# Attention and a routed MoE on one core: conditions nested, block products back to back, three weight loads moved

## The chip, the cores and the metric

The kernel runs on one core of one Trainium2 chip. The metric is device time in microseconds (us) of one launch. Five engines run side by side, each with its own stream of instructions: PE (TensorE, the matrix products), DVE (VectorE), ACT (ScalarE), POOL (GpSimd) and SP (SyncE, which here only issues DMA transfers). They wait for one another through semaphores.

## The reference

Local and global attention (4 batches, 8 heads, 512 local and 32 global rows, head size 64) gives 2176 rows of 512 numbers. These rows go through a mixture of 8 experts; each row goes to one expert, up to `capacity` rows for each.

```python
logits = x @ w_gate
expert_idx = np.argmax(logits, axis=1)
gate_w = probs[np.arange(N), expert_idx]
# row i becomes row counts[e] of its expert's disp[e], while counts[e] < capacity
h = np.maximum(np.einsum('ecd,edf->ecf', disp, w1), 0.0)
y = np.einsum('ecf,efd->ecd', h, w2)
out[i] = gate_w[i] * y[expert_idx[i], pos[i]]
```

`w1` is 512 x 1024 and `w2` 1024 x 512 for each expert.

## The kernel before

Up to about 140 us a planner with hand-written costs places the attention; the change doesn't touch it. Behind it come the experts, in a stretch where the order written in the code is the order on each engine (`tc.manual_schedule()`). How many rows an expert has is known only at run time, so an expert is coded as blocks of 128 rows, 3 for expert 0 and 4 for every other, and block `i` > 0 runs only under the condition `nb[e] > i`, where `nb[e]` is read from the table of counts. Block 0 always runs. The first two blocks of rows of expert 0 that were ready earlier (`y1`) are done ahead of this.

With the inputs of this case the blocks that run are 2, 3, 2, 3, 2, 1, 4, 1 for experts 0 to 7: 18 in all. The row counts of the trace agree: 576 products with `wl` at 32 a block.

Products are made of 16-bit halves. A weight w becomes `wh` (its rounded value) and `wl` (the rest), x and h likewise. A block is two products:

- `up(e, i)`: two groups of 48 matmuls, each into one PSUM tile `pa` of the ring `psA` (5 tiles, handed out in code order, counting blocks that don't run). Behind each group `relu` writes `hh` on ACT (L990) and `hl` on DVE (L991), which frees the tile. Each matmul has a weight load of its own, so an `up` is 192 instructions on PE.
- `down(e, i)`: 24 matmuls (48 instructions) into a tile `py`, then `scale` on DVE (L998, even i) or ACT (odd i) into the row buffer `ys`, then `send`, an indirect DMA of POOL that scatters the rows to the output.

Beside this run the preparations for later experts. `w_next(k)` issues a load of 1 MB raw weights on SP (chunk k belongs to expert k // 4). `split(n)` takes n halves of chunks: `wh` on ACT (L933), then `wl` on DVE (L934), eight halves for an expert, and a `w_next` behind each second one. The buffers of `wh`, `wl` alternate between two experts, so the first half for expert e+1 can be written only after the last product of expert e-1. `gather(e)` collects the rows of expert e by indirect DMAs of POOL (L945) into `xg`, and `turn(e)` transposes them by DMAs of SP (L963) into `xT`. `count(e)` reads `nb[e]`.

In the kernel before, every `up` and `down` of a block i > 0 has a condition of its own (`guard`, L1048), and the products are staggered: `down(e, i+1)` stands behind `up(e, i)`, and `down(e-1, 0)` behind `up(e, n-1)`, where n is the coded number of blocks. A condition that isn't met is a jump on each engine; the jumped part also raises the semaphores that its instructions would have raised, once the engine's own earlier work is done.

Of the kernel before, what the change touches and what calls it, by code (L numbers as in the profile page):

```python
# [9 lines left out]
F32 = mybir.dt.float32  # L10
# [4 lines left out]
ET = mybir.EngineType  # L15
PSUM = bass.MemoryType.PSUM

B, H, SL, SG, HD = 4, 8, 512, 32, 64
S = SL + SG
NTOK = B * S  # L20
DM, FF, NE = 512, 1024, 8
HP = H // 2
NT = 20
# [874 lines left out]
def experts(tc, weigh, head, ident, x16d, sidx, gslot, didx, cnts, w1, w2, ws, w_split, wp0, rp, out):  # L898
    nc = tc.nc
    with ExitStack() as ctx:  # L900
# [18 lines left out]
        def w_next(k):  # L919
            if 0 <= k < 4 * NE:  # L920
                w_load(k // 4, k % 4)
# [19 lines left out]
        def flag(i, engines):  # L941
            return nc.values_load(cnts[0:1, i:i + 1], engines=engines, min_val=0, max_val=1)  # L942
# [28 lines left out]
        def gemm1(ps, wt, x, ft):  # L971
            wh, wl = wt
            m = 0
            for kc in range(4):
                s = slice((kc % 2) * FF + 128 * ft, (kc % 2) * FF + 128 * ft + 128)
                for wx, xi in ((wh, 0), (wh, 1), (wl, 0)):
                    nc.tensor.matmul(ps, wx[:, kc // 2, s], x(2 * kc + xi), start=(m == 0), stop=(m == 11))  # L977
                    m += 1

        def wide(py, wt, h):  # L980
            wh, wl = wt
            m = 0
            for ft in range(8):
                s = slice((ft % 4) * DM, (ft % 4) * DM + DM)
                for i, wx in ((0, wh), (1, wh), (0, wl)):
                    nc.tensor.matmul(py, h(i, ft), wx[:, 2 + ft // 4, s], start=(m == 0), stop=(m == 23))  # L986
                    m += 1

        def relu(hh, hl, ps):
            nc.scalar.activation(hh, ps, AF.Relu)  # L990
            nc.vector.scalar_tensor_tensor(out=hl, in0=ps, scalar=0.0, in1=hh, op0=ALU.max, op1=ALU.subtract)  # L991

        def scale(yo, e, i, py, n=128):
            gs = gslot[0:n, NBLK * e + i:NBLK * e + i + 1]
            if i % 2:
                nc.scalar.activation(yo[0:n], py[0:n], AF.Copy, scale=gs)
            else:
                nc.vector.tensor_scalar_mul(yo[0:n], py[0:n], gs)  # L998

        def store(src, idx):  # L1000

            r = nc.gpsimd.indirect_dma_start(  # L1002
                out=out[:, :], out_offset=IndirectOffsetOnAxis(ap=idx, axis=0), in_=src, in_offset=None,
                bounds_check=NTOK - 1, oob_is_err=False,
            )
            tc.declare_no_dep(r.ins, group="rows", reason="each token's row is written once")
            tc.add_to_no_dep_group("rows", r.ins)

        def send(yo, e, i, n=128):
            store(yo[0:n], sidx[0:n, e, i:i + 1])  # L1010

        def hidden(name):
            return [hpool.tile([128, 8, 128], F16, tag=f"h{x}", name=f"h{x}{name}") for x in "hl"]
# [3 lines left out]
        def blocks(e):  # L1017
            return 3 if e == 0 else 4

        def up(e, i):  # L1020
            H[e, i] = hidden(f"{e}_{i}")

            def work():
                for g in range(2):
                    ps = psA.tile([128, 4, 128], F32, tag="a", name="pa")
                    for f in range(4):
                        gemm1(ps[:, f, :], ws[e], lambda k: xT[e][:, k, 128 * i:128 * i + 128], 4 * g + f)
                    f = slice(4 * g, 4 * g + 4)
                    relu(H[e, i][0][:, f, :], H[e, i][1][:, f, :], ps[:])

            guard(e, i, work)

        def down(e, i):
            yo = yos[(4 * e + i) % len(yos)]

            def work():
                py = psY.tile([128, 512], F32, tag="y", name="py")
                wide(py, ws[e], lambda x, ft: H[e, i][x][:, ft, :])
                scale(yo, e, i, py)

            guard(e, i, work)
            send(yo, e, i)

        def guard(e, i, work):
            if i == 0:
                work()
            else:
                with tc.If(nb[e] > i):  # L1048
                    work()

        todo = []
        yos = [yp.tile([128, DM], F32, name=f"ys{i}", bufs=1) for i in range(6)]
# [1 line left out]
        def split(n):  # L1054
            for e, c, h in todo[:n]:
                w_half(e, c, h)
                if h:
                    w_next(4 * e + c + 6)
            del todo[:n]
# [5 lines left out]

        def expert(e):

            n = blocks(e)
            if e + 1 < NE:
                w_pair(e + 1)  # L1070
                todo.extend((e + 1, c, h) for c in range(4) for h in range(2))
            for i in reversed(range(n)):
                up(e, i)
                split(1)
                if i == n - 1:
                    if e:
                        down(e - 1, 0)
                        if e == 1:
                            for j in range(HEAD):
                                store(y1[j][:], head["sidx"][:, j:j + 1])  # L1080
                    if e == 2:
                        with tc.If(flag(2 * NE, (ET.Pool,)) > 0):
                            for t in range(NT):
                                store(zero[:], didx[:, t:t + 1])
                    if e + 2 < NE:
                        gather(e + 2)
                        count(e + 2)
                else:
                    down(e, i + 1)
                    if i == 0 and e + 2 < NE:  # L1090
                        turn(e + 2)
                split(1)
            split(len(todo))

        def beyond(e):
            M = CAP - ROWS
# [20 lines left out]
            send(yo, e, 4, M)  # L1117

        with tc.manual_schedule():
            for k in range(4, 9):  # L1120
                w_next(k)
            gather(0)
            turn(0)
            gather(1)
            nc.gpsimd.memset(zero, 0.0)
            for t in yos:
                nc.gpsimd.memset(t, 0.0)
            weigh(None)
            y1 = []
            for i in range(HEAD):  # L1130
                py = psY.tile([128, 512], F32, tag="y", name="py")
                wide(py, ws[0], lambda x, ft: head["hl" if x else "hh"][:, ft, 128 * i:128 * i + 128])
                if i == 0:
                    weigh(psY.tile([128, 2, NE * NBLK], F32, tag="y", name="tg"))
                y1.append(yp.tile([128, DM], F32, tag=f"yo{i}", name=f"yo{i}", bufs=1))
                nc.vector.tensor_scalar_mul(y1[i], py, head["gslot"][:, i:i + 1])
            count(0)
            count(1)
            turn(1)
            w_next(9)  # L1140
            for e in range(NE):
                expert(e)
            down(NE - 1, 0)
            with tc.If(flag(2 * NE + 1, ALL) > 0):
                for e in range(NE):
                    beyond(e)
# [93 lines left out]
```

## Time and profile before

| | us |
|---|---|
| three runs | 391.24, 384.72, 389.38 |
| median | 389.38 |
| the profiled execution, device time | 386.15 |
| its span (first to last instruction) | 384.4 |
| PE busy | 332.4 (86%) |
| DVE busy | 221.6 (58%) |
| ACT busy | 186.4 (48%) |
| POOL busy | 174.2 (45%) |

The profiled execution is 1.75 us longer than its span and 3.2 us below the median. The trace gives for each engine the instructions with start and duration, and for an idle time the engine or transfer whose event ended it ("<-"); "PEq" and "DVEq" are the engines' sequencers, whose branch instructions don't count as busy.

### The profile page before, as it was taken

The page shows a single profiled execution, that of the slowest core. Times are in us where ns is not written, and L with a number is a line of the kernel's source. Part 1 is how long each engine was busy: PE and PEld are TensorE (multiplying, and loading weights), DVE is VectorE, ACT ScalarE, POOL GpSimd, SP SyncE. Part 2 cuts the span into 40 slices and gives each one's busy share as a digit, 9 for nine tenths or more (in the row PEclk, how much of TensorE's full clock was granted, in tenths as well). Part 3 has the DMA queues.
Part 4 walks back from the last instruction along what each step waited for, and adds up shares of the span by engine and source line. Part 5 has one row for each costly group of instructions (what it writes and reads, how often), then busy time and mean ns, then how long its engine had stood idle before and what let it go on. Part 6 is the DMA issues. An engine that isn't in the chain of part 4 may idle for free. (4 is left out here: it accounts for less than half of the span.)

```text
span 384.4 us, 12011 instructions
## 1 busy us (share of the span) xinstructions
PE 332.4 (86%) x4788; PEld 230.6 (60%) x4788; DVE 221.6 (58%) x679; ACT 186.4 (48%) x369; POOL 174.2 (45%) x235
## 2 busy tenths in 40 slices
PE   6978997897988999499999999999997399999870
PEld 2455565575565785295777594975673397776540
DVE  3678979979788976333654373642672643342220
ACT  2778988778858722034542552623443433333100
POOL 8657878777575143074661126530251720200410
PEclk9799989999998999789999999999999599999996
DMA  8999895556464649759999776746399940000100
GB/s 215 286 242 362 195 262 143 142 173 211 113 196 138 106 128 398 202 110 292 235 388 319 180 272 198 254 143 147 139 374 212 341 71 2 35 21 29 59 7 9
DMA packets 62730, 70.61 MB, mean 184 GB/s; under 512 B 33598, under 2 KB 41918, under 8 KB 62656
## 3 DMA queue, kind: packets, MB, share of 16 engines
q1 hardware_dynamic: 57232, 60.32, 56.6%
q0 software_dynamic: 5280, 8.93, 6.6%
q8 instruction: 52, 0.85, 0.9%
q10 hardware_dynamic: 144, 0.33, 0.3%
q14 instruction: 22, 0.18, 0.2%
HBM read 59.06 MB, written 13.11 MB: 188 GB/s over the span
## 5 line engine op out<-in xcount | busy, mean ns | idle before, releaser
L977 PE MATMUL pa<-xT,wh 128*128 128x128 f16 x1152 | 102.4, 223 | 19.4 <-DVEq L1048 10.0
L977 PEld LDWEIGHTS <-wh 128*128 128x128 f16 x1152 | 91.2, 100 | 24.3 <-DVEq L1048 11.0
L977 PE MATMUL pa<-xT,wl 128*128 128x128 f16 x576 | 101.1, 223 | 0.0
L934 DVE SCALAR_TENSOR_TENSOR wl<-raw,wh 128x1024 f16<-128x1024 f32 x56 | 67.8, 1223 | 54.9 <-ACT wh L933 31.0
L1002 POOL DMA_INDIRECT out_dram<-ys,sidx x31 | 39.9, 1289 | 115.6 <-DVE ys L998 54.4
L933 ACT ACTIVATE wh<-raw 128x1024 f16<-128x1024 f32 x56 | 57.2, 1049 | 23.0 <-PE py L986 20.4
L990 ACT ACTIVATE hh<-pa 128x512 f16<-128x512 f32 x36 | 21.5, 596 | 91.3 <-PE pa L977 87.5
L986 PE MATMUL py<-wh,hh 128*128 128x512 f16 x176 | 64.1, 379 | 1.1
L986 PE MATMUL py<-wl,hh 128*128 128x512 f16 x160 | 60.6, 379 | 0.0
L237 POOL COPY vt<-vt 32x520 f32<-32x520 f32 (+1 forms) x80 | 52.2, 652 | 13.4 <-DMA vt<-in_v_dram 8.4
L977 PEld LDWEIGHTS <-wl 128*128 128x128 f16 x576 | 57.8, 100 | 0.0
L986 PEld LDWEIGHTS <-hh 128*128 128x128 f16 x336 | 32.6, 98 | 40.8 <-issue 4.0
L986 PE MATMUL py<-wh,hl 128*128 128x512 f16 x144 | 54.6, 379 | 0.0
L991 DVE SCALAR_TENSOR_TENSOR hl<-pa,hh 128x512 f16<-128x512 f32 x36 | 24.7, 689 | 49.6 <-ACT hh L990 47.6
L945 POOL DMA_INDIRECT xg<-x16d,sidx x31 | 33.0, 1064 | 36.4 <-DMA xT<-xg 17.9
L277 ACT ACTIVATE P<-P,nb 128x128 f32<-128x128 f32 x128 | 43.3, 394 | 9.8 <-DVE nb L270 9.2
L261 PE MATMUL s<-kbd,qt 128*32 128x256 f32 x512 | 37.8, 420 | 4.2 <-DMA kbd<-in_k_dram 2.2
L270 DVE CUSTOM_DVE_ANT_0 P<-s,cf 128x128 f32<-128x128 f32 x128 | 30.6, 283 | 9.9 <-PE s L261 9.6
L295 PE MATMUL xo<-vt,ptr 128*32 128x65 f32 x1024 | 22.1, 224 | 4.6 <-issue 2.4
L261 PEld LDWEIGHTS s<-kbd,qt 128*32 128x32 f32 x512 | 15.5, 117 | 16.6 <-issue 6.6
L323 POOL TENSOR_TENSOR x<-x,x 128x512 f16<-128x512 f32 x14 | 17.9, 1277 | 14.9 <-ACT x L320 13.3
L295 PEld LDWEIGHTS xo<-vt,ptr 128*32 128x32 f32 x1024 | 17.4, 111 | 9.6 <-issue 4.4
(152 smaller groups left out, 412.6 us busy)
## 6 DMA issues: line engine op xcount, KB each, us to landing
raw<-in_w_dram SPq DMA_DIRECT2D x32, 1024.0 KB, 7.1
vt<-in_v_dram SPq DMA_DIRECT2D x16, 390.0 KB, 5.1
kbd<-in_k_dram SPq DMA_DIRECT2D x32, 168.0 KB, 5.0
qt<-in_q_dram SPq DMA_DIRECT2D x16, 256.0 KB, 5.3
x16d<-x SPq DMA_DIRECT2D x16, 256.0 KB, 2.5
x16d<-x16g SPq DMA_DIRECT2D x32, 8.0 KB, 3.0
xg<-x16d,sidx POOLq DMA_INDIRECT x31, 5.4
out_dram<-ys,sidx POOLq DMA_INDIRECT x31, 4.6
```

Of the source, the lines that this page charges most:

```text
L237: eng.tensor_copy(dst, src)
L261: nc.tensor.matmul(s[32 * c:32 * c + 32, 2 * i:2 * i + 2, :], qt[u][:, 32 * t:32 * t + 32], kt[u][:, :, o:o + 128], start=True, stop=True,)
L270: nc.vector.tensor_tensor_reduce(out=P[u, g][:, j, :], in0=ps["s", u, g][:, j, :], in1=mask[:, 2 * g + j // 2, :], scale=-0.125, scalar=3e ...
L277: nc.scalar.activation(p, p, AF.Exp, scale=-1.0, bias=ps["nb", u, h][:, j:j + 1])
L295: nc.tensor.matmul(x[cs, j, :], ps["pt", u, g][:, j, cs], vt[u][:, w, j % 2, :], start=True, stop=True)
L933: nc.scalar.activation(wh[:, c, s], raw[e, c][:, s], AF.Copy, scale=SW)
L934: nc.vector.scalar_tensor_tensor(out=wl[:, c, s], in0=raw[e, c][:, s], scalar=SW, in1=wh[:, c, s], op0=ALU.mult, op1=ALU.subtract)
L945: nc.gpsimd.indirect_dma_start(out=dst[0:n], out_offset=None, in_=x16d[:, :], in_offset=IndirectOffsetOnAxis(ap=sidx[0:n, e, i:i + 1], axi ...
L977: nc.tensor.matmul(ps, wx[:, kc // 2, s], x(2 * kc + xi), start=(m == 0), stop=(m == 11))
L986: nc.tensor.matmul(py, h(i, ft), wx[:, 2 + ft // 4, s], start=(m == 0), stop=(m == 23))
L991: nc.vector.scalar_tensor_tensor(out=hl, in0=ps, scalar=0.0, in1=hh, op0=ALU.max, op1=ALU.subtract)
L1002: r = nc.gpsimd.indirect_dma_start(out=out[:, :], out_offset=IndirectOffsetOnAxis(ap=idx, axis=0), in_=src, in_offset=None, bounds_check=N ...
```

## The change

Each expert now has one nest of conditions: `nb[e] > 1` outermost, inside it `nb[e] > 2`, inside it `nb[e] > 3`; on the way out stand `up` and `down` of the block, back to back (`more`, whose conditions show as L1040). Block 0 follows with `up(e, 0)` and `down(e, 0)`. The sends of blocks 3 to 1, `gather(e+2)` and `count(e+2)` stand between `more` and `up(e, 0)`, and so does `ahead(e+1)`, which marks on PE where the next expert's conditions may be announced. The splits are taken as 2, 2, 3 and 1 instead of one by one. Of the five raw loads ahead of expert 0's gathers and transposes, three now stand behind its transposes.

```diff
-            guard(e, i, work)
+        def more(e, i):
+
+            if i < blocks(e):
+                with tc.If(nb[e] > i, label=f"b{e}_{i}"):
+                    more(e, i + 1)
+                    up(e, i)
+                    down(e, i)
+
+        def ahead(e):
+            if e < NE:
+                for i in range(1, blocks(e)):
+                    tc.mark_branch_hint_location(f"b{e}_{i}", hint=nb[e] > i, engines=[ET.PE])
...
-            for i in reversed(range(n)):
-                up(e, i)
-                split(1)
-                if i == n - 1:
-                    if e:
-                        down(e - 1, 0)
...
-                else:
-                    down(e, i + 1)
-                    if i == 0 and e + 2 < NE:
-                        turn(e + 2)
-                split(1)
-            split(len(todo))
+            split(2)
+            more(e, 1)
+            split(2)
+            for i in reversed(range(1, blocks(e))):
+                send(row(e, i), e, i)
...
+            if e + 2 < NE:
+                gather(e + 2)
+                count(e + 2)
+            ahead(e + 1)
+            up(e, 0)
+            if e + 2 < NE:
+                turn(e + 2)
+            split(3)
+            down(e, 0)
+            send(row(e, 0), e, 0)
+            split(1)
...
         with tc.manual_schedule():
-            for k in range(4, 9):
+            for k in range(4, 6):
                 w_next(k)
             gather(0)
             turn(0)
+            for k in range(6, 9):
+                w_next(k)
             gather(1)
...
             for e in range(NE):
                 expert(e)
-            down(NE - 1, 0)
```

SP around the transposes of expert 0, before (L44 and L47 are the raw loads, L963 the transposes):

```order
L44 DMA raw_1_3280<-in_w_dram 128x2x1024
L47 DMA raw_2_3282<-in_w_dram 128x4x512
L47 DMA raw_3_3284<-in_w_dram 128x4x512
L44 DMA raw_0_3286<-in_w_dram 128x2x1024
L963 DMA_TRANSPOSE xT_3288<-xg_2_3291 128x8x128
L963 DMA_TRANSPOSE xT_3288<-xg_1_3290 128x8x128
L963 DMA_TRANSPOSE xT_3288<-xg_0_3289 128x8x128
```

The same place on SP after:

```order
L44 DMA raw_1_3280<-in_w_dram 128x2x1024
L963 DMA_TRANSPOSE xT_3282<-xg_2_3285 128x8x128
L963 DMA_TRANSPOSE xT_3282<-xg_1_3284 128x8x128
L963 DMA_TRANSPOSE xT_3282<-xg_0_3283 128x8x128
L47 DMA raw_2_3303<-in_w_dram 128x4x512
L47 DMA raw_3_3305<-in_w_dram 128x4x512
L44 DMA raw_0_3307<-in_w_dram 128x2x1024
```

Three loads, 3 MB, have passed from ahead of the transposes to behind them.

DVE from expert 4 to expert 5, before (the digit behind a name is the expert, the next one the block or chunk; L991 is relu's half, L934 the split's, L998 `scale`):

```order
L934 SCALAR_TENSOR_TENSOR wl5_5830<-raw5_3_5539,wh5_5829 128x1024
L1048 COMPARE_AND_BRANCH
L991 SCALAR_TENSOR_TENSOR hl5_3_6442<-pa_6444,hh5_3_6441 128x512
L991 SCALAR_TENSOR_TENSOR hl5_3_6442<-pa_6495,hh5_3_6441 128x512
L1048 UNCONDITIONAL_BRANCH x2
L934 SCALAR_TENSOR_TENSOR wl6_6440<-raw6_0_5680,wh6_6439 128x1024
L998 TENSOR_SCALAR ys4_3274<-py_6548,gslot_67 128x512
L1064 TENSOR_LOAD cnts_69
L934 SCALAR_TENSOR_TENSOR wl6_6440<-raw6_0_5680,wh6_6439 128x1024
L1048 COMPARE_AND_BRANCH
```

The same place on DVE after:

```order
L998 TENSOR_SCALAR ys4_3274<-py_6466,gslot_67 128x512
L934 SCALAR_TENSOR_TENSOR wl5_5884<-raw5_3_5672,wh5_5883 128x1024
L934 SCALAR_TENSOR_TENSOR wl6_6500<-raw6_0_5846,wh6_6499 128x1024 x2
L1040 COMPARE_AND_BRANCH x3
L991 SCALAR_TENSOR_TENSOR hl5_3_6511<-pa_6512,hh5_3_6510 128x512
L991 SCALAR_TENSOR_TENSOR hl5_3_6511<-pa_6563,hh5_3_6510 128x512
```

`scale` of `down(4, 0)`, the last split half for expert 5 and the first two for expert 6 now all stand ahead of DVE's first condition of expert 5; before, one split half and a condition alternated.

PE at the border of experts 4 and 5, before (L986 is `down`, L977 `up`):

```order
L986 MATMUL py_6399<-wl4_5220,hh4_1_6151 128x512
L1048 UNCONDITIONAL_BRANCH x2
L1048 COMPARE_AND_BRANCH
L977 LDWEIGHTS wh5_5829
L977 MATMUL pa_6444<-xT5_5357,wh5_5829 128x128
```

PE after: first the row ahead of `up(4, 0)` and then, 240 rows on, the border itself:

```order
L986 MATMUL py_6258<-wl4_5268,hh4_1_6154 128x512
L1040 UNCONDITIONAL_BRANCH x2
L1063 TENSOR_LOAD cnts_69
L1063 ISA x2
L1048 REGISTER_ALU
L1236 BRANCH_PREFETCH_HINT
L977 LDWEIGHTS wh4_5267
```

```order
L986 MATMUL py_6466<-wl4_5268,hh4_0_6347 128x512
L1040 COMPARE_AND_BRANCH x3
L977 LDWEIGHTS wh5_5883
L977 MATMUL pa_6512<-xT5_5683,wh5_5883 128x128
```

There is one announcement (BRANCH_PREFETCH_HINT) for each of experts 1 to 7, for the outermost condition and one block of products ahead of it; the two inner conditions have none, nor has expert 0. The three comparisons stand together at the border.

## Rows read from the trace of the kernel before

**Rows 1.** Five stretches of the span from the end of the work ahead of expert 0 to the end: start and end, length, then busy us and instructions of PE, PEld (weight loads), DVE, ACT and POOL, the granted clock of PE, the busy share of the DMA engines, GB/s.

```profile
155.79:161.48 5.69, 0.00 (x0) 0.00 (x1) 3.11 (x3) 0.00 (x0) 0.00 (x0) 0.74 0.83 180
161.48:295.85 134.37, 130.43 (x1440) 93.80 (x1440) 65.42 (x68) 54.76 (x68) 55.09 (x51) 0.99 0.80 233
295.85:304.12 8.27, 0.00 (x0) 0.00 (x1) 6.79 (x7) 5.93 (x6) 4.29 (x4) 0.66 1.11 260
304.12:372.86 68.74, 66.24 (x720) 48.20 (x720) 23.40 (x26) 18.21 (x24) 14.79 (x13) 0.97 0.17 50
372.86:384.37 11.51, 0.00 (x0) 0.00 (x0) 0.75 (x1) 0.00 (x0) 0.98 (x1) 0.68 0.03 9
```

**Rows 2.** What PE waited for between 150 and 384 us: who waited, what ended it, us in all, how often, the longest.

```profile
PE pa L977 <- DVEq L1048: 10.0, 2, 8.3
PE pa L977 <- DMA xT<-xg: 5.7, 1, 5.7
PE pa L977 <- PEq L1048: 3.2, 6, 0.9
```

**Rows 3.** PE's instructions in order of time, those that follow a break at the start of an expert: start, duration, operation, and in brackets the idle time before it and what ended it.

```profile
161.48 0.40 PE L977 MATMUL pa<-xT,wh 128*128 128x128 f16 x2 [5.69 <-DMA xT<-xg]
...
190.97 0.27 PE L977 MATMUL pa<-xT,wh 128*128 128x128 f16 x2 [0.43 <-PEq L1048]
...
218.44 0.28 PE L977 MATMUL pa<-xT,wh 128*128 128x128 f16 x2 [0.74 <-PEq L1048]
...
273.83 0.28 PE L977 MATMUL pa<-xT,wh 128*128 128x128 f16 x2 [0.95 <-PEq L1048]
...
304.12 0.40 PE L977 MATMUL pa<-xT,wh 128*128 128x128 f16 x2 [8.28 <-DVEq L1048]
...
361.83 0.27 PE L977 MATMUL pa<-xT,wh 128*128 128x128 f16 x2 [1.77 <-DVEq L1048]
```

**Rows 4.** PE again: the first products of two `up`s of expert 6, two blocks apart, and the seam between the last `up` of expert 7 and its `down`.

```profile
322.79 0.28 PE L977 MATMUL pa<-xT,wh 128*128 128x128 f16 x2
...
343.87 0.28 PE L977 MATMUL pa<-xT,wh 128*128 128x128 f16 x2
...
367.15 0.22 PE L977 MATMUL pa<-xT,wl 128*128 128x128 f16 x1
367.52 0.38 PE L986 MATMUL py<-wh,hh 128*128 128x512 f16 x1
```

**Rows 5.** The stretches behind the two long breaks of PE, columns as in rows 1.

```profile
161.48:165.20 3.72, 3.72 (x36) 3.72 (x37) 0.00 (x0) 0.00 (x0) 1.58 (x2) 0.50 0.19 38
304.12:308.70 4.58, 4.58 (x44) 4.58 (x45) 1.04 (x1) 0.00 (x0) 3.67 (x4) 0.50 1.00 366
```

**Rows 6.** Expert 0's supply in order of time: SP's issues of the three loads that the change moves and of the transposes (SPq), then POOL's first and third gather; then two stretches, columns as in rows 1; last, over all transfers of `xg` from 140 to 200 us, the time from issue to landing.

```profile
141.63 1.38 SPq L47 DMA_DIRECT2D raw<-in_w_dram  x2
143.05 1.83 SPq L44 DMA_DIRECT2D raw<-in_w_dram  x1
156.73 4.03 SPq L963 DMA_TRANSPOSE xT<-xg  x3
...
146.86 1.07 POOL L945 DMA_INDIRECT xg<-x16d,sidx  x1 [2.81 <-DVE dl L460]
...
149.54 1.00 POOL L945 DMA_INDIRECT xg<-x16d,sidx  x1 [0.30 <-issue]
...
142.00:148.00 6.00, 6.00 (x59) 4.08 (x58) 5.33 (x27) 1.20 (x3) 2.60 (x4) 1.00 0.93 377
148.00:154.00 6.00, 6.00 (x46) 3.17 (x45) 2.46 (x10) 2.00 (x2) 2.00 (x2) 1.00 1.05 390
...
DMA to landing us min/median/max: 2.4/3.5/7.7
```

**Rows 7.** DVE around the starts of experts 5 and 7, and ACT and DVE at expert 7's last relu, columns as in rows 3.

```profile
296.75 1.22 DVE L934 SCALAR_TENSOR_TENSOR wl<-raw,wh 128x1024 f16<-128x1024 f32 x1 [3.42 <-ACT wh L933]
297.90 0.74 DVE L998 TENSOR_SCALAR ys<-py,gslot 128x512 f32<-128x512 f32 x1
298.56 1.21 DVE L934 SCALAR_TENSOR_TENSOR wl<-raw,wh 128x1024 f16<-128x1024 f32 x1
299.99 2.36 DVE L934 SCALAR_TENSOR_TENSOR wl<-raw,wh 128x1024 f16<-128x1024 f32 x2 [0.21 <-DVEq L1048]
...
360.10 0.75 DVE L998 TENSOR_SCALAR ys<-py,gslot 128x512 f32<-128x512 f32 x1 [2.55 <-PE py L986]
...
367.40 0.60 ACT L990 ACTIVATE hh<-pa 128x512 f16<-128x512 f32 x1 [2.08 <-PE pa L977]
...
368.03 0.69 DVE L991 SCALAR_TENSOR_TENSOR hl<-pa,hh 128x512 f16<-128x512 f32 x1 [1.99 <-ACTq L1048]
```

**Rows 8.** DMA packets of queue q8, which carries instructions, in the break before expert 5 (295.85 to 304.12 us) and in the 8 us that end just behind the start of expert 7 (354 to 362 us): packets, MB, share of 16 engines.

```profile
q8 instruction: 2, 0.03, 1.6%
...
q8 instruction: 2, 0.03, 1.5%
```

**Rows 9.** Expert 6's supply: POOL's last gather for it, SP's transposes of it, and the raw load that SP issues behind them.

```profile
282.11 0.99 POOL L945 DMA_INDIRECT xg<-x16d,sidx  x1 [0.31 <-issue]
...
288.89 7.22 SPq L963 DMA_TRANSPOSE xT<-xg  x4
296.21 1.50 SPq L44 DMA_DIRECT2D raw<-in_w_dram  x1
```

More of the change, by code (lines that the diff above doesn't have):

```diff
@@ L1021, in up, with row @@
             H[e, i] = hidden(f"{e}_{i}")
[L1023 to L1029, printed above, removed]
-            guard(e, i, work)
-        def down(e, i):
[L1034 to L1046, printed above, removed]
-            else:
-                with tc.If(nb[e] > i):
-                    work()
+            for g in range(2):
+                ps = psA.tile([128, 4, 128], F32, tag="a", name="pa")
+                for f in range(4):
+                    gemm1(ps[:, f, :], ws[e], lambda k: xT[e][:, k, 128 * i:128 * i + 128], 4 * g + f)
+                f = slice(4 * g, 4 * g + 4)
+                relu(H[e, i][0][:, f, :], H[e, i][1][:, f, :], ps[:])
+        def row(e, i):
+            return yos[(4 * e + i) % len(yos)]
+        def down(e, i):
+            py = psY.tile([128, 512], F32, tag="y", name="py")
+            wide(py, ws[e], lambda x, ft: H[e, i][x][:, ft, :])
+            scale(row(e, i), e, i, py)
+        def more(e, i):
[8 more added lines that the diff above has]
+                    tc.mark_branch_hint_location(f"b{e}_{i}", hint=nb[e] > i, engines=[ET.PE])
         todo = []
@@ L1066, in expert @@
         def expert(e):
-            n = blocks(e)
             if e + 1 < NE:
@@ L1071, in expert @@
                 todo.extend((e + 1, c, h) for c in range(4) for h in range(2))
-            for i in reversed(range(n)):
-                up(e, i)
-                split(1)
-                if i == n - 1:
-                    if e:
-                        down(e - 1, 0)
[L1078 to L1088, printed above, removed]
-                    down(e, i + 1)
-                    if i == 0 and e + 2 < NE:
-                        turn(e + 2)
-                split(1)
-            split(len(todo))
+            split(2)
[3 more added lines that the diff above has]
+                send(row(e, i), e, i)
+            if e == 1:
+                for j in range(HEAD):
+                    store(y1[j][:], head["sidx"][:, j:j + 1])
+            if e == 2:
+                with tc.If(flag(2 * NE, (ET.Pool,)) > 0):
+                    for t in range(NT):
+                        store(zero[:], didx[:, t:t + 1])
+            if e + 2 < NE:
[9 more added lines that the diff above has]
+            split(1)
         def beyond(e):
```

## The prediction

> **What bounds the kernel now.** I read the stretches first. From 161.48 us to 372.86 us PE is busy nearly all the time except for one hole of 8.27 us; ahead of it is a hole of 5.69 us, behind it a tail of 11.51 us in which only the last rows are written [rows 1]. DVE, ACT and POOL have spare time in the same stretches, about half or more. So PE sets the end of the expert stage, and a change is worth what it takes from PE's breaks, from time at the low clock, or from the moment at which PE can begin. The list of PE's waits names the breaks: 5.7 us for the transposes of expert 0, 10.0 us in two waits with DVE's sequencer named, 3.2 us in six waits for PE's own sequencer [rows 2]. PE's rows place them: 5.69 before expert 0, .43 at expert 1, .74 at expert 2, .95 at expert 4, 8.28 at expert 5 and 1.77 at expert 7 [rows 3].
>
> To size what is lost I take undisturbed work from the same trace. From 322.79 to 343.87 two blocks go by, 10.54 us each [rows 4]. An undisturbed `up` is 361.83 to 367.37, 5.52 or so, and the `down` behind it 367.52 to 372.86, 5.34 [rows 1, 3, 4]; start to end these would be 10.86, and matmuls that overlap at a seam of unlike products give .16 back at each of two seams. 18 blocks at 10.54 are 189.7 us; the stage took 211.4. [...]
>
> DVE is named for the 8.28 us, but I don't believe it. By the code order of the PSUM ring, the first group of `up(5, 0)` needs the tile that DVE passes over in the jumped `up(5, 3)`, and DVE was at 296.75 already in the split half behind that place, some 7 us before PE went on [rows 7]. What stands at this place on PE are four jumps over 480 instructions. The same four jumps stand at expert 7, where the hole is 1.77. In both stretches two packets of instructions were fetched [rows 8], while the DMA engines carried 260 GB/s around the first and a mean of 50 over the stretch that holds the second [rows 1]. So I read both holes as PE waiting for its code, dear when the DMA engines are full. At experts 2 and 4 two jumps over 240 instructions cost .74 and .95 under full traffic.
>
> **The change part by part.**
>
> *The three raw loads.* They are issued on SP at 141.63 to 143.05, ahead of the gathers, whose issues run from 146.86 to 149.54; the third lands when the first transpose goes off, at 156.73, 7.2 us after its issue [rows 6]. Meanwhile the DMA engines are full at 377 and 390 GB/s. Three loads are 3.1 MB, 8 us of that traffic. Without them a gather of about the median 3.5, or 2.4 at best, is at hand [rows 6], so the transposes go off at 152.0 to 153.0; I take 152.6, **4.1 us earlier**. The bounds are 0 (the gathers are slow for another reason) and 4.8. PE then starts at 157.4, 1.6 us after the work ahead of it ended at 155.79. A break of 1.77 at expert 7 left the clock at its high level, those of 5.69 and 8.28 didn't [rows 1, 3, 5], so **1.84 us** of low clock go too. Bounds of this part together: 0 to 6.6. The three loads themselves are wanted by the splits of experts 1 and 2, ten and more us later, behind PE work; on SP they pass only the three transposes. If they came too late, DVE would be late, not PE, up to some 3 us.
>
> *Products back to back.* `down` directly behind its own `up` could wait for relu. At expert 7 it did so before the change: the `up` ends at 367.37, `down` starts at 367.52, while `hh` of the second group was written from 367.40 to 368.00 and `hl` from 368.03 to 368.72 [rows 4, 7]. The first quarter of `down` needs the first group only. I cost this at nothing; the cover is the 2.7 us that `down` takes for its first four slices, against .60 + .69 of relu. Like products now meet nowhere inside an expert, so the seams fall from 4.1 us to none: **4.1 gained** (bounds 2 and 4.1).
>
> *The nest and its new wait.* Conditions go from two a block to one. But ahead of the first condition of an expert DVE now has `scale` of `down(e-1, 0)`, the last split half of this expert and the first two of the next. `scale` starts when `down` ends; the steps from row to row are .66, 1.15 and 1.22 for such instructions and .21 for the passage over conditions [rows 7], so DVE passes the condition .03 + .66 + 1.15 + 1.22 + 1.22 + .21 = **4.5 us after PE's last product**. Until then the jumped blocks' PSUM tiles aren't free, and queued behind the two splits on DVE are the relus of the first block that runs. Who waits is PE. With two blocks (experts 2 and 4) the first group of `up(e, 1)` has a tile and runs 2.76 us, the second waits: 4.5 - 2.76 = 1.74 each, where .74 + .30 and .95 + .30 were lost. With one block (expert 5) the first group itself waits: 4.5, and the clock may fall again; I take 1.84, between 0 (the 1.77 row) and 2.19 (the 8.28 row). At expert 7 no splits of a next expert are left: scale, one split half and the passage, about 2.4, in place of 1.77. With three blocks (1 and 3) I keep the .43 of the row at expert 1. Sum of what is lost after: 2 x 1.74 + 4.5 + 1.84 + 2.4 + 2 x .43 = **13.1**; of before, without the seams and expert 0's clock: 21.7 - 4.1 - 1.84 = 15.8. The nest gives **2.7 us**, less about 1.3 that I allow for overlaps at the borders that a break swallows.
>
> *Jumps.* The announcement covers expert 5's and 7's jump, now a single one over 726 instructions, because there the outermost condition fails. Experts 2 and 4 jump at the second condition, over 484 instructions, twice the distance of before, and unannounced. If the code takes F us to come, the loss there is the larger of 1.74 and F. The nearest rows: .95 (half the distance, full traffic) and, as far above, 8.28 (the same distance in four jumps, full traffic). I take F under 1.74, since a single jump over the same distance with idle DMA engines would be at most the 1.77 of four; F of 4 would add 2.3 at each.
>
> [...]
>
> Sum: 4.1 + 1.84 + 4.1 + 2.7 - 1.3 = 11.4 us. The profiled execution's 386.15 becomes 374.7. The three runs' median lies 3.2 above this execution, and I don't know whether the code fetches that the change shortens are what varies, so I add 2: **377 us**.
>
> **The rivals.**
>
> *A. The long unannounced jumps at experts 2 and 4 wait for code.* For it: the two holes with packets in them, full traffic at both places. Against it: .95 at 240 instructions. At F = 4, half of 8.28 since one jump stands for four, 2 x 2.3 = 4.6 more, and about 1 more at experts 1 and 3, if those also cost .95: 382 to 383.
>
> *B. The waits only move.* The gathers land late for another reason, the gain at the start is 0 to 2, and the wait for DVE at the borders eats the rest: 377 + 4 to 6, plus up to 4 when the clock falls at experts 2 and 4 too: 382 to 387. For it: the gathers' longest 7.7 is a property of many rows; against it, the full DMA engines in just those 6 us.
>
> *C. Slower: raw loads come late behind the transposes of SP.* `turn(e+2)` waits for `gather(e+2)`, which on POOL now stands behind the sends of blocks 3 to 1, and these wait for their `scale`. Each SP transfer behind it, the raw loads of `split(3)`, waits along. Before, the last gather for expert 6 was issued at 282.11, the transposes went off from 288.89, and the raw load behind them at 296.21 [rows 9]. The gathers move back by up to one block, 10.5 us; I find 3 to 4 us of slack for expert 6's raw load. It decides for slower only when it is late by more than 11 us, or when both jumps of A cost 8.28: then 2 x 6.5 = 13 of the 11.4 are lost, 388 to 392.
>
> *D. It doesn't do what it says*: only the outermost condition is announced, and if that has no effect the hole at expert 5 stays 8.28 instead of 4.5, and its clock 2.19: 4.1 more, 381.
>
> *E. Better:* DVE gets to the splits sooner, expert 5's break is short enough to keep the clock, and code is no matter: 370 to 373.
>
> **How the numbers follow.** Two per cent of 389.4 is 7.8 us, about what a measurement of this kernel can tell from no change; faster means under 381.6, slower over 397.2. Chances: the forecast .42 (373 to 381), E .10, D .10 (379 to 383), A .20 (380 to 385), B .12 (382 to 387), C .06 (388 to 400). Faster: .42 + .10 + half of D .05 + a fifth of A .04 = .61; slower: only the far end of C, with what I have overlooked, .05; same .34. The range leaves out the better half of E and C: 371 to 387.
>
> **What would show it.** In the changed kernel's rows: the third gather lands by 153, PE starts expert 0 at 157 to 158 with the clock at its high level; no break between `up` and its `down`; at experts 2 and 4 a break of 1.7 in the middle of the first `up` that DVE ends; at expert 5 a break of 4.5 in place of 8.28. A break ahead of the first `up` of experts 2 and 4, ended by PE's sequencer and with instruction packets in it, would be A. A transposed tile or a split that PE waits for would be C. It is wrong if the announced jump still costs 8 us, or if gathers at the start land 7 us after issue with less traffic.

## Result and profile after

In 20 interleaved runs each, the changed kernel took 382.61 us (median, 374.1 to 389.06) and the kernel before 387.14 us (384.22 to 391.3). The ratio is **0.9745, 95% interval 0.9694 to 0.9796**. The ratio compares only the runs within 1.5% of each kernel's fastest, 6 of 20 for the changed kernel and 18 of 20 for the kernel before, so it says 9.9 us where the medians of all runs say 4.5. The forecast was 377, with a range of 371 to 387. On two other chips the same kernel gave 0.9824 (0.9746 to 0.9902) and 0.9779 (0.9707 to 0.9851); there the medians fell by 8.1 and 5.7 us.

The profiled execution took 381.53 us, its span is 379.6 where it was 384.4. The stretches that answer to [rows 1], columns as there:

```profile
158.63:160.62 1.99, 0.00 (x0) 0.00 (x0) 0.82 (x2) 0.00 (x0) 0.00 (x0) 1.00 1.08 103
160.62:296.57 135.95, 129.25 (x1440) 93.84 (x1440) 65.86 (x69) 54.31 (x68) 59.18 (x51) 0.99 0.77 239
296.57:300.88 4.31, 0.00 (x2) 0.01 (x1) 4.15 (x4) 3.83 (x4) 2.94 (x2) 1.00 0.27 62
300.88:368.13 67.25, 65.21 (x720) 47.70 (x720) 26.62 (x29) 19.99 (x26) 17.06 (x15) 0.97 0.37 106
368.13:379.60 11.47, 0.00 (x0) 0.00 (x0) 0.75 (x1) 0.00 (x0) 0.98 (x1) 0.69 0.03 9
```

The work ahead of expert 0 ended 2.84 us later than in the trace of before (158.63 against 155.79), in a part that the change doesn't touch. From there the break ahead of expert 0 fell from 5.69 to 1.99, the stage of the experts from 211.38 to 207.51, and the tail is the same. 2.84 - 3.70 - 3.87 - .04 = -4.77, which is the 4.8 between the spans.

PE's waits after, to hold against [rows 2]:

```profile
PE pa L977 <- DVEq L1040: 6.3, 2, 4.3
PE pa L977 <- PEq L1040: 4.7, 3, 2.3
PE pa L977 <- DMA xT<-xg: 2.0, 1, 2.0
PE pa L977 <- issue: 1.8, 2, 1.6
```

And where they are, against [rows 3] (start, duration, operation, idle time before it and what ended it):

```profile
160.62 0.23 PE L977 MATMUL pa<-xT,wh 128*128 128x128 f16 x1 [2.00 <-DMA xT<-xg]
...
183.81 0.22 PE L977 MATMUL pa<-xT,wh 128*128 128x128 f16 x1 [0.30 <-PEq L1040]
...
186.51 0.23 PE L977 MATMUL pa<-xT,wl 128*128 128x128 f16 x1 [1.59 <-issue]
...
219.48 0.22 PE L977 MATMUL pa<-xT,wh 128*128 128x128 f16 x1 [2.12 <-PEq L1040]
...
222.50 0.22 PE L977 MATMUL pa<-xT,wl 128*128 128x128 f16 x1 [0.24 <-issue]
...
275.33 0.22 PE L977 MATMUL pa<-xT,wh 128*128 128x128 f16 x1 [2.28 <-PEq L1040]
...
300.88 0.28 PE L977 MATMUL pa<-xT,wh 128*128 128x128 f16 x1 [4.31 <-DVEq L1040]
...
357.41 0.23 PE L977 MATMUL pa<-xT,wh 128*128 128x128 f16 x1 [2.04 <-DVEq L1040]
```

These are experts 0, 1 (twice), 2 (twice), 4, 5 and 7. Expert 1, which jumped once over 242 instructions, stops .30 at its start and 1.59 more after 1.11 us of its first `up`; the second stop waits for nothing that the profile shows. I read it as missing code; no run shows that by itself. Experts 2 and 4 stop for 2.12 and 2.28 where they stopped for .74 and .95. Expert 5 stops for 4.31 instead of 8.28. The seams inside a block and between blocks are overlaps now, of .16 or .17, but for one break of .15 at the jump of expert 3.

### The profile page after: what moved, and what is told of

Its sections match the earlier page's. It is cut to its first block, busy times and chain, and to the rows that moved or that the text cites. A ratio compares the mean times of both kernels' runs of the same rounds, so it can differ in the third digit from the quotient of the medians.

```text
span 379.6 us, 11865 instructions
## 1 busy us (share of the span) xinstructions
PE 326.7 (86%) x4788; PEld 229.8 (61%) x4788; DVE 220.6 (58%) x679; ACT 185.4 (49%) x369; POOL 178.5 (47%) x235
## 5 line engine op out<-in xcount | busy, mean ns | idle before, releaser
L977 PE MATMUL pa<-xT,wh 128*128 128x128 f16 x1152 | 101.9, 223 | 13.2 <-DVEq L1040 6.3
L977 PEld LDWEIGHTS <-wh 128*128 128x128 f16 x1152 | 90.9, 100 | 19.5 <-DVEq L1040 7.3
L977 PE MATMUL pa<-xT,wl 128*128 128x128 f16 x576 | 100.5, 222 | 1.8 <-issue 1.8
L934 DVE SCALAR_TENSOR_TENSOR wl<-raw,wh 128x1024 f16<-128x1024 f32 x56 | 65.5, 1220 | 36.6 <-ACT wh L933 35.2
L1002 POOL DMA_INDIRECT out_dram<-ys,sidx x31 | 37.3, 1203 | 103.1 <-ACT ys L996 45.1
L986 PE MATMUL py<-wh,hh 128*128 128x512 f16 x176 | 64.1, 379 | 0.0
L986 PE MATMUL py<-wl,hh 128*128 128x512 f16 x160 | 60.6, 379 | 0.0
L991 DVE SCALAR_TENSOR_TENSOR hl<-pa,hh 128x512 f16<-128x512 f32 x36 | 24.8, 690 | 59.0 <-ACT hh L990 56.8
L977 PEld LDWEIGHTS <-wl 128*128 128x128 f16 x576 | 57.5, 100 | 1.8 <-issue 1.8
L945 POOL DMA_INDIRECT xg<-x16d,sidx x31 | 40.6, 1310 | 36.4 <-DMA xT<-xg 18.0
L933 ACT ACTIVATE wh<-raw 128x1024 f16<-128x1024 f32 x56 | 55.2, 1046 | 4.8 <-PE py L986 3.5
L986 PEld LDWEIGHTS <-hh 128*128 128x128 f16 x336 | 32.7, 98 | 36.8
L986 PE MATMUL py<-wh,hl 128*128 128x512 f16 x144 | 54.6, 379 | 0.0
L261 PE MATMUL s<-kbd,qt 128*32 128x256 f32 x512 | 34.0, 387 | 4.1 <-DMA kbd<-in_k_dram 3.2
L261 PEld LDWEIGHTS s<-kbd,qt 128*32 128x32 f32 x512 | 14.7, 111 | 14.0 <-issue 5.9
```

Source lines behind the costliest of these rows:

```text
L261: nc.tensor.matmul(s[32 * c:32 * c + 32, 2 * i:2 * i + 2, :], qt[u][:, 32 * t:32 * t + 32], kt[u][:, :, o:o + 128], start=True, stop=True,)
L933: nc.scalar.activation(wh[:, c, s], raw[e, c][:, s], AF.Copy, scale=SW)
L934: nc.vector.scalar_tensor_tensor(out=wl[:, c, s], in0=raw[e, c][:, s], scalar=SW, in1=wh[:, c, s], op0=ALU.mult, op1=ALU.subtract)
L945: nc.gpsimd.indirect_dma_start(out=dst[0:n], out_offset=None, in_=x16d[:, :], in_offset=IndirectOffsetOnAxis(ap=sidx[0:n, e, i:i + 1], axi ...
L1002: r = nc.gpsimd.indirect_dma_start(out=out[:, :], out_offset=IndirectOffsetOnAxis(ap=idx, axis=0), in_=src, in_offset=None, bounds_check=N ...
```

## Experiments

The kernels ran in three groups of four, each group on one chip beside the kernel before. The chip of the first group was slower with everything: the kernel before took 401.9 us there. The changed kernel itself didn't run on that chip.

**The loads alone, twice.** Only the move of the three loads, on the kernel before:

```diff
-            for k in range(4, 9):
+            for k in range(4, 6):
                 w_next(k)
             gather(0)
             turn(0)
+            for k in range(6, 9):
+                w_next(k)
```

> The kernel before with the three raw loads moved behind expert 0's transposes and nothing else. Theory (the full DMA engines held up the gathers): the third gather lands 2.2 us or so after the last issue instead of 7.2, PE's break ahead of expert 0 falls from 5.7 to about 2.0, and nothing else changes; 3.7 us faster, and 1.6 more only if the clock stays high behind the shorter break: 382 to 384 where the kernel before stands at 387. Rival (the gathers are slow by themselves, or the loads are missed later): no change, 386 to 388, with a break for a split at expert 1.

Measured: 395.31 us against 401.9, ratio 0.9793 (0.9714 to 0.9871). PE's break ahead of expert 0 was 2.4, and its first `up` took 7.16, as long as the 7.17 in the trace of after, whose first 3.58 us had a clock of .55 (below).

> The loads alone. Theory A: 3 to 5 us faster than the kernel before and as much slower than the changed one. Theory B: 5 to 8 us faster than the kernel before, within 2 us of the changed one; in its trace expert 5 still has a hole of 4.5 to 8, which splits into 4.0 up to DVE's passage and a rest.

Measured in the third group: 385.53 against 387.86, ratio 0.9941 (0.9900 to 0.9983): 2.3 us, less than either theory had. The trace has the break at 1.78, the first `up` at 5.54 and this at expert 5:

```profile
298.21 0.40 PE L977 MATMUL pa<-xT,wh 128*128 128x128 f16 x2 [8.02 <-DVEq L1048]
```

In that kernel DVE took up its next split behind the conditions at 294.34, 4.1 us after PE's last product at 290.20. So of the 8.02 some 4.1 lie ahead of DVE's passage and 3.9 behind it.

**The nest alone, twice.** The changed kernel with the loads in the old order:

```diff
-            for k in range(4, 6):
+            for k in range(4, 9):
                 w_next(k)
             gather(0)
             turn(0)
-            for k in range(6, 9):
-                w_next(k)
```

> The changed kernel with its raw loads in the old order, so the nest, the order of the products and the announcements alone. Theory: the break ahead of expert 0 is 5.7 again and its first up at the low clock takes 7.4; from there the stage is 4 us shorter than before, from the seams (4) and expert 5 (4), less what the jumps at experts 1, 2 and 4 cost more (about 4): 382 to 385. Rival (loads and nest are worth something only together, because a start moved forward meets later transfers): 386 to 388.

Measured: 403.2 against 401.9, ratio 0.999 (0.9947 to 1.0034). On this chip `down` did wait for its own relu, nearly all of it in block 0 of three experts, 4.4 us in all; so it did without announcements (below), in block 0 of four experts, 6.6 us. One of these rows, from the trace without announcements:

```profile
325.71 0.39 PE L986 MATMUL py<-wh,hh 128*128 128x512 f16 x1 [1.76 <-ACT hh L990]
```

The loads alone, which keep the staggered order, have no such wait on that chip.

> The nest alone. Theory A: 3 to 5 us faster than the kernel before. Theory B: within 2 us of it, with breaks of about 1.9, 2.4 and 1.1 to 2.3 at experts 1, 2 and 4 that PE's own code ends, and no like seams.

Measured in the third group: 387.57 against 387.86, ratio 0.9988 (0.9942 to 1.0034). Twice the nest alone is worth nothing. Its trace has the forecast overlaps at every seam but one, and expert 5's hole at 4.30; and it has 1.98, 2.58 and 1.47 at experts 1, 2 and 4. The break ahead of expert 0 was 6.43, and the first `up` behind it took 8.33. The trace is of the longest of its twelve runs; its stage took 209.70.

**No announcements, twice.**

```diff
-            ahead(e + 1)
```

> The changed kernel without its announcements. Theory (the hole at expert 5 was PE fetching code, and the announcement took it away): expert 5's break grows from 4.3 to 6 to 9 us and is ended by PE's own code, expert 7's from 2.0 to 2.5 or more, experts 2 and 4 stay at 2.1 to 2.3: 2 to 5 us slower than the changed kernel. Rival (the hole was a wait for DVE all along, and the announcement does nothing): 4.3 and 2.0 as with it, the same time.

Measured: 397.78 against 401.9, ratio 0.9899 (0.9836 to 0.9961). Expert 5's break was 5.32, and just as long in the two kernels of that group that announce (nest alone, and inner conditions announced): DVE reached the condition 5.2 us after PE's last product in all three. Expert 7 had 2.04.

> The changed kernel without announcements. If announcing hides the code of the jumps at experts 5 and 7, these breaks grow by 1 us or more over those of the changed kernel and the time by 2 to 5. If DVE's passage of the conditions is what PE waits for there, PE starts within .2 us of DVE's passage with or without announcements, and the time is within 2 us of the changed kernel.

Measured in the third group, beside the changed kernel: 383.0 and ratio 0.982 (0.9755 to 0.9886), where the changed kernel had 382.14 and 0.9779. Experts 5 and 7 stop for 4.31 and 2.04, the same as with announcements. One thing differs at expert 5:

```profile
301.96 0.28 PE L977 MATMUL pa<-xT,wh 128*128 128x128 f16 x2 [4.31 <-DVEq L1040]
...
303.92 0.39 PE L977 MATMUL pa<-xT,wh 128*128 128x128 f16 x2 [1.61 <-issue]
```

PE began on DVE's passage and then stood 1.61 us; no engine or transfer is named as the one it waited for. Behind it PE started 9 or 10 matmuls in each microsecond from 304 to 309, and 17 or 18 in the two after them. In the trace of after the clock was .52 in the first 3.52 us of this `up` and 1.00 in the rest. So the slow pace lasted longer, and this first `up` took 9.80 us where the three traces of the changed kernel have 7.16. So announcing takes away at most 2.6 us at expert 5 by this trace; in the first group's trace without announcements no such stop stands there (first `up` 7.63). The times can't tell it from nothing.

**Inner conditions announced.**

```diff
                 with tc.If(nb[e] > i, label=f"b{e}_{i}"):
-                    more(e, i + 1)
+                    ahead(e, i + 1)
                     up(e, i)
                     down(e, i)
+                    more(e, i + 1)
...
```

> The changed kernel with the inner conditions behind their block instead of ahead of it (block 1, then block 2 inside, then block 3 inside that), each announced on PE one block ahead of its jump. Theory (PE waits for code where a jump over 242 or 484 instructions is unannounced): the breaks of 1.9, 2.4 and 2.3 at experts 1, 2 and 4 fall to .4 or less, expert 5 keeps the wait of 4.3 for DVE; 5 to 6 us faster than the changed kernel, and less spread from run to run. Rival (a jump costs its 2 us announced or not): the breaks move behind block 1 and the time stays.

Measured: 405.55 against 401.9, ratio 1.0016 (0.9948 to 1.0083). The rival held: the breaks at the starts of experts 1, 2 and 4 are gone, as the theory said, but wherever a jump now stands behind a block there is a new one. At expert 0 it is 1.33, at experts 1 and 3 it is 1.55, ended by DVE; at experts 2 and 4, behind block 1, it is this:

```profile
239.24 0.27 PE L977 MATMUL pa<-xT,wh 128*128 128x128 f16 x2 [1.50 <-issue]
...
301.06 0.22 PE L977 MATMUL pa<-xT,wh 128*128 128x128 f16 x1 [1.45 <-issue]
```

So PE stood 1.5 at an announced jump over 484 instructions, where it stood .8 to 2.9 at an unannounced one in the other traces. That needn't be the price of the jump: the engine that scales the block ahead passes the same condition only behind that `scale`. At expert 2 this is ACT, whose next work starts at 238.79, .45 ahead of PE; at expert 4 it is .41, and at experts 1 and 3, with DVE in ACT's place, .36 and .35. Whether PE waited for that engine or for code isn't shown. PE's waits held an item that was larger here than anywhere: stops between matmuls that nothing explains, 15.0 us in 28 (those at the jumps among them).

```profile
PE pa L977 <- issue: 15.0, 28, 1.5
```

The `up` of expert 1's block 0 (208.17 to 220.81) shows them microsecond by microsecond, columns as in rows 1:

```profile
210.00:211.00 1.00, 1.00 (x22) 1.00 (x19) 0.23 (x1) 0.00 (x0) 0.73 (x1) 1.00 0.56 184
...
212.00:213.00 1.00, 0.49 (x3) 0.13 (x2) 0.00 (x0) 0.00 (x0) 0.70 (x2) 1.00 0.75 156
213.00:214.00 1.00, 0.39 (x4) 0.23 (x4) 0.00 (x0) 0.00 (x0) 0.89 (x1) 1.00 1.04 358
214.00:215.00 1.00, 0.35 (x4) 0.23 (x5) 0.00 (x0) 0.00 (x0) 0.80 (x1) 1.00 0.90 274
215.00:216.00 1.00, 0.49 (x5) 0.15 (x3) 0.00 (x0) 0.00 (x0) 0.69 (x2) 1.00 1.06 420
...
218.00:219.00 1.00, 0.34 (x4) 0.18 (x2) 0.61 (x1) 0.35 (x1) 0.00 (x0) 0.50 0.35 112
```

PE has 22 records of matmuls in a microsecond while the DMA engines have a share of .56, and 3 to 5 in the four rows with .75 to 1.06. No engine is named as the one it waits for. I read it as code that trickles in beside full DMA engines; that is read from the coincidence, not tried by itself, and the last row, with 4 records at a share of .35, doesn't fit it.

**The changed kernel again, twice.** No edit.

> The changed kernel once more, for a second trace of it beside the others on one chip. Theory (announcements as such cost or gain at most 1 us a place): it stands 10 to 15 us below the kernel before and below the variant without announcements. Rival (PE runs out of code while the DMA engines are full, in rows of matmuls with .3 to .5 us between them, and announcing makes this worse): it stands above the variant without announcements, whose ratio to the kernel before was .990, and its trace shows such rows at experts 1, 2, 4 or 5.

Measured: 380.01 against 388.11, ratio 0.9824. By medians it stands 8.1 below the kernel before, short of the theory's 10 to 15. No rows of stops; PE lost 1.98, 3.12 and 1.47 at experts 1, 2 and 4. The low clock behind expert 0's break, which was 2.02, did not occur this time (first `up` 5.53).

> The changed kernel on one chip with its two halves and with the variant without announcements. Theory A (the start is worth about 4 us, the nest about as much): 0.978 to 0.985 of the kernel before, 3 to 5 us below the loads alone and the nest alone. Theory B (the nest gives back at the jumps of experts 1, 2 and 4 what it saves at the seams): within 2 us of the loads alone.

Measured: 382.14 against 387.86, ratio 0.9779. By medians, on that one chip: loads alone -2.3, nest alone -.3, both -5.7. The two don't add up; the 3 us between are less than the spread of each of these kernels' runs (8 to 9 us), so whether the two help one another stays open. On the chip of the first group the loads alone came to 6.6 below the kernel before, and loads and nest without announcements to only 4.1: what the nest adds isn't settled.

**The kernel before again.** No edit.

> The kernel before once more, for a trace of it on the same chip as the others. Theory (PE's code comes late when the DMA engines are full): its trace, too, has rows of matmuls with .3 to .5 us between them at some of the experts, and a hole of 5 to 9 us at expert 5; how much of this there is differs from trace to trace, by some 10 us in all. Rival (such rows belong to the nest and to the announcements): it has none, and its stage from expert 0 to the end lasts 211 us as in its first trace.

Measured: 388.52, ratio 0.9983 (0.9915 to 1.005). The rows of stops aren't there; the stage took 212.46 us and expert 5's hole was 7.97. The work ahead of expert 0 ended at 157.86.

**The kernel before with quiet DMA engines.** Chunks 6 to 11 serve in place of 12 to 31.

```diff
...
+            k = 4 * e + c
+            if k >= 12 and (e, c) not in raw:
+                raw[e, c] = raw[(6 + k % 6) // 4, (6 + k % 6) % 4]
+                return
...
```

> The kernel before without the raw loads of chunks 12 to 31: the weights of experts 3 to 7 are not fetched, and the splits take chunks that are there already, so DVE, ACT and PE do the same work on other numbers with little DMA traffic from 190 us on. Theory (the hole of 8.3 us at expert 5 is code that comes late because the DMA engines are full): it falls to the 1.8 of expert 7, the jumps at expert 4 cost .5 or less, and no rows with gaps are left: the stage is 8 to 12 us shorter. Rival (the hole is a wait for DVE's order): it stays at 5 to 8.3 us, and at most the .3 us for a split goes.

Measured: 383.26 against 388.11, ratio 0.9913 (0.9861 to 0.9965). The stage took 208.27, 4.2 less than in the kernel before on that chip, and nearly all of it is the hole at expert 5. PE and DVE there:

```profile
303.94 0.29 PE L981 MATMUL pa<-xT,wh 128*128 128x128 f16 x1 [3.99 <-DVEq L1052]
```

```profile
302.00 0.74 DVE L1002 TENSOR_SCALAR ys<-py,gslot 128x512 f32<-128x512 f32 x1
302.66 5.09 DVE L938 SCALAR_TENSOR_TENSOR wl<-raw,wh 128x1024 f16<-128x1024 f32 x4
```

The first split of DVE's row ends at 302.66 + 1.22 = 303.88, and PE starts at 303.94. Both theories were half right: 4.0 of the hole is a wait for DVE to pass a condition behind that split, and the other 3.9 to 4.4 isn't there in this run, where the DMA engines moved a mean of 41 GB/s (299.5 to 306) and not the 278 of before (295 to 306). It isn't that a helper came later: DVE's row starts 2.71 us after PE's last product here and in the trace of before, and ACT and POOL, too, stand where they stood. Code is the reading that is left to me; this run doesn't show it by itself. The jumps at expert 4 stayed at .86.

**All four splits behind the nest.**

```diff
-            split(2)
             more(e, 1)
-            split(2)
+            split(4)
```

> The changed kernel with the first two split halves behind the nest instead of ahead of it (all four behind it). Theory (DVE passes the conditions 4.3 us after PE's last product because two split halves stand ahead): DVE passes at about 2.1 us, expert 5's break of 4.3 falls to 2.1 and its first up runs at the high clock; 3 to 4 us faster than the changed kernel. Rival (code is late there anyway): the break stays over 4 us and is put down to PE's own sequencer, the time stays, or it grows where the later splits make a down wait.

Measured: 392.6 against 388.11, ratio 1.0131 (1.0036 to 1.0227): slower than the kernel before by 0.4 to 2.2%, where 3 to 4 us less than the changed kernel were forecast. What the theory said of the break at expert 5 came true to a tenth; that the clock would stay high behind it did not (first `up` 7.17, where 5.53 goes with a clock of 1.00, below):

```profile
304.87 0.75 DVE L998 TENSOR_SCALAR ys<-py,gslot 128x512 f32<-128x512 f32 x1 [1.24 <-PE py L986]
305.53 1.22 DVE L934 SCALAR_TENSOR_TENSOR wl<-raw,wh 128x1024 f16<-128x1024 f32 x1
306.96 2.36 DVE L934 SCALAR_TENSOR_TENSOR wl<-raw,wh 128x1024 f16<-128x1024 f32 x2 [0.21 <-DVEq L1040]
```

```profile
306.86 0.23 PE L977 MATMUL pa<-xT,wh 128*128 128x128 f16 x1 [2.04 <-DVEq L1040]
```

DVE passes right behind one split and PE starts with it, 2.04 us after its last product. But the four splits now stand ahead of the relus of `up(e, 0)`, and `down(e, 0)` waits for `hl` in six of the experts:

```profile
PE py L986 <- DVE hl L991: 8.9, 6, 1.5
```

Besides, the first `up` behind each of the breaks of 2.0 to 2.9 at experts 0, 2, 4, 5 and 7 took 7.1 to 7.2 here. Wherever the two splits stand, PE waits for them: ahead of the nest it costs 2.3 us at one expert, behind it 1.5 at six.

## Why the prediction was right, and where its steps failed

The direction and the range held. The sum rests on a loss of 21.7 us in the stage of before, 211.4 less 189.7. The trace of before shows its parts: 13.6 of breaks; 4.0 of clock, from first `up`s of 7.36 at expert 0 and 7.71 at expert 5, which began at a clock of .50, against 5.52 undisturbed (1.84 and 2.19 more); and a rest of 4.1, put down to seams of like products, which show breaks of .15 (at 168.99 and 179.84, say) where unlike ones overlap by .16. By the first trace of each kernel the change gave 7.6 us, 3.7 ahead of expert 0 and 3.9 behind it, where my sum had 11.4: two thirds of it. The 3.8 that are missing are mainly 2.3 at the jumps of experts 1 to 4 and 1.6 of clock behind expert 0's break. The median, 382.61, lies outside the 373 to 381 that I called likeliest and in the 380 to 385 of rival A, and the 2.3 were lost where A has its loss, most of them at expert 1. That the range held is owed to its width, too: the kernel before alone spreads over 7 us. Term by term, with the three traces of the changed kernel:

- **The raw loads, 4.1: nearly right.** The first transpose went off 7.2 us after the last gather's issue before, and 2.15 after (154.54 behind 152.39, below); with 4.05 in another trace of the changed kernel. PE's break was 1.99, 2.02 and 3.92 against 5.7, so 3.7, 3.7 and 1.8 were gained. The loads alone brought 2.4 and 1.8. In the nine traces with the loads moved the break was 1.8 to 2.4 in six and 3.9 to 4.2 in three; why the three differ is open.

```profile
154.54 4.00 SPq L963 DMA_TRANSPOSE xT<-xg  x3
...
152.39 1.00 POOL L945 DMA_INDIRECT xg<-x16d,sidx  x1 [0.30 <-issue]
```

- **The clock behind it, 1.84: wrong in two traces of three.** I argued from the 1.77 of expert 7 that a break of 1.6 keeps the clock. The break came out at 2.0 in two traces, and there it goes either way: the granted clock was .55 behind 1.99 in the one and 1.00 behind 2.02 in the other. In the third the break was 3.92 and the first `up` took 7.89, against 5.53 at the clock of 1.00.

```profile
160.62:164.20 3.58, 3.58 (x37) 3.58 (x38) 2.29 (x2) 0.00 (x0) 1.77 (x2) 0.55 1.03 366
```

```profile
160.69:164.20 3.51, 3.51 (x63) 3.51 (x64) 2.28 (x2) 0.56 (x1) 1.76 (x2) 1.00 1.05 377
```

- **Back to back, nothing: right.** In the traces of the changed kernel no `down` waited for relu; all `up` to `down` seams in the trace of after overlap by .16 or .17. It isn't safe: on the chip of the first group such waits came to 4.4 and 6.6 us in the two kernels with the nest named above. **The seams, 4.1: right.** One break of .15 is left, at the jump of expert 3.
- **The wait for DVE: right at experts 5 and 7.** Forecast 4.5 and 2.4; measured 4.31 and 2.04, and the clock (.52 in the first 3.52 us of that `up`) cost 1.64 where I took 1.84. In the trace of after DVE ends its third split at 297.28 + 3.49 = 300.77, and PE starts at 300.88:

```profile
297.28 3.49 DVE L934 SCALAR_TENSOR_TENSOR wl<-raw,wh 128x1024 f16<-128x1024 f32 x3
300.98 2.36 DVE L934 SCALAR_TENSOR_TENSOR wl<-raw,wh 128x1024 f16<-128x1024 f32 x2 [0.21 <-DVEq L1040]
```

- **The same wait at expert 4: right in form.** I had the loss there as the larger of 1.74 and F, with a break in the middle of the first `up` that DVE ends. Where the jump was short, this is what stands there, 1.08 and then .39 in the second trace:

```profile
273.40 0.27 PE L977 MATMUL pa<-xT,wh 128*128 128x128 f16 x2 [1.08 <-PEq L1040]
...
276.63 0.28 PE L977 MATMUL pa<-xT,wh 128*128 128x128 f16 x2 [0.39 <-DVEq L1040]
```

  The second break ends 4.31 after PE's last product, as at expert 5. The sum is 1.47 here, and again in the third group's nest alone (.88 and .59) and without announcements (.77 and .70): the floor is 1.47 where I had 1.74.
- **What the hole of 8.28 was: wrong by half.** I took the whole of it for code, because I had PE wait for the tile of the jumped `up(5, 3)`; the run with quiet DMA engines shows it waiting for DVE to pass the next condition, behind `scale` and one more split. The wait for DVE of 4.0 was there before the change. So the change didn't bring a new wait at expert 5; it moved the old one by .3 and took away what came on top of it. That the hole shrank to 4.3 was right for a reason that I had only in part, and so partly by luck.
- **The jumps at experts 1, 2 and 4: too cheap.** I took F under 1.74, hidden by the wait for DVE, and .43 at expert 1. The traces show 1.9, 2.0 and 1.6 lost at expert 1, 2.4, 3.1 and 2.2 at expert 2 and 2.3, 1.5 (the floor above) and 1.8 at expert 4. Expert 1 alone is 1.4 above my term; and the break of 2.21 at expert 2 was followed by a clock of .53 and a first `up` of 7.15 in one trace. This is rival A, at F = 1.1 to 2.5 and not the 4 that I gave it. By its trace in the third group this also takes a good part from the nest alone: saved at seams and at expert 5, paid at three jumps and at the clock. That it is all of why the nest alone stands at 0.999 isn't shown. Nor is it shown that these breaks are PE waiting for code: no releaser but PE's own sequencer, or none, is named, the jumps at expert 4 didn't shrink with quiet DMA engines, and announcing them moved the breaks and didn't take them away.

The breaks go with the distance of the jump in part, .74 and .95 over 240 instructions and .8 to 2.9 over 484. But over 242 expert 1's jump cost 1.6 to 2.1 and expert 3's .15, so distance isn't all of it.

- **The likeliest single figure**, 377, is 5.6 below the median, in spite of the 2 us that I added for it. The spread was not foreseen: 374 to 389, where before had 384 to 391. Part of both is the work ahead of expert 0, which ended between 154.8 and 161.1 in the ten traces of this case that don't come from the slow chip, with no order by kernel. On top of it the changed kernel has three or four breaks of about 2 us behind which the clock falls in some executions and not in others (.55 behind 1.99 and 1.00 behind 2.02 at expert 0), 1.64 us each; how much of the spread that is no run shows.
- **D** is half true: only the outermost conditions are announced, and this brings at most 2.6 us. **C** didn't occur: no wait of PE for a split's product or a transposed tile after expert 0.

On the two chips where the changed kernel ran beside variants, none of them beat it.

## What to carry to other kernels

A jump over an `If` wasn't free here to those who wait on the other engines: DVE came to the condition by its own order, and what stood ahead of it there was paid by PE, which skipped the block. At expert 5 that was 4.31 us with `scale` and three split halves ahead of the condition, and 2.04 with `scale` and one (all four splits behind the nest). Moving bulk loads behind a small transfer that the bottleneck waits for was cheap here and shortened its break in every trace, from 5.7 to between 1.8 and 4.2. Merging the conditions traded several short jumps for fewer long ones, and three of these cost more than the short ones had: 1.9, 2.4 and 2.3 us in the trace of after, at experts 1, 2 and 4, against .43, .74 and .95 at their starts before. Read a hole's releaser together with that engine's own time: where it had passed 4 us earlier, as in the kernel before, a second cause follows the first.

## What the runs showed of the hardware

I had not expected that breaks of the same length differ in what they do to the clock: it was .55 behind 1.99 and .53 behind 2.21, and 1.00 behind 2.02, 2.04 and 2.28. Leaving out the slow chip: behind breaks of 1.76 to 1.83 the next `up` took 5.5 to 5.7. Behind breaks of 2.0 to 2.9 it took 5.5 to 5.7 in some traces, stops left out, and 7.1 to 7.2 in others. Behind 3.9 and more it always took 7.1 or more.

Nor that PE's stops between matmuls differ that much between chips: on the slowest chip (401.9 us for the kernel before) every trace had rows of matmuls with gaps of .3 to .5. All stops there that nothing explains come to 4.7 to 15.0 us a trace, those at jumps among them, against .3 to 3.6 in the other traces of these kernels that have any. In the row shown above (inner conditions announced, 211 to 219) the share of the DMA engines was .35 to 1.06, .84 on average. That such stops need busy DMA engines isn't shown. One or two stops of about .3 stand at expert 7 as well (.28 without announcements, .30 with the inner conditions announced).
